# Weight copies issued one step later behind the attention's stores, and the order of seven products

## The chip, the cores and the metric

The kernel runs on one core of a Trainium2 chip. The metric is the device time of one execution in microseconds (us). Engines are named as in the profile: PE (matrix products), PEld (its weight loads), DVE and POOL (vector work), ACT (activations and copies) and SP, which in this kernel computes nothing and issues nearly all the DMA transfers, in the order in which they are written. L909 is line 909 of the kernel before.

## The reference

Two blocks follow each other. Attention keeps, of each row of scores, the 32 largest:

```python
scores = scale * q @ k.T                                  # 8 x 8 heads, 576 x 576, head size 64
mask   = scores >= (32nd largest of the row)
attn   = softmax(where(mask, scores, -1e9))
x      = (attn @ v), heads side by side                   # 8 x 576 x 512
```

Then comes a Fourier mixing and an MLP with two layers:

```python
u   = x + real(fft(fft(x, axis=1), axis=2))
un  = (u - mean(u)) / sqrt(var(u) + 1e-6)
out = u + relu(un @ w_ch1) @ w_ch2                        # 512 -> 2048 -> 512
```

All of it is float32; the output is 8 x 576 x 512.

## The kernel before

**Steps.** The attention is cut into 288 items (`items`, `N` = 288), each up to 128 rows of one head's scores; two heads form a pair, a pair has 9 items, and a batch element has 4 pairs, or 36 items. The loop at L1492 makes one step of each item. Step i does on DVE the 32-largest search of item i (eight passes, L425 and L427), on PE the scores of item i+3, and on ACT and POOL the masking of item i-1 (`mask`, L448 and L451) and its exponentials (`expo`, L459).

**P and its transposes.** The weights after the exponential are called P. For most pairs P is transposed by DMA: `plane` (called at L1560 and L1561 for item i-2) has ACT copy P into two planes of 16 bits (L472) and has SP store them in DRAM (L485, or L488 for the item of the tails); `turn` (L1557, for item i-3, every second item) has SP issue a DMA transpose from DRAM into the tile PT (L506). `attend` (L555, matmuls on L564) multiplies PT by v; it comes last of PE's work in its step. The result goes through ACT (`attended`), is turned back by PE in `to_tokens` (matmuls on L604) and normalised by DVE (L608). So DVE waits at L608 for everything that PE has in front of L604.

**The MLP rides along.** The MLP of a batch element runs in the steps of the next one, in units of about 1.75 us of PE, which a planner (`level`, `some`) puts between the fixed PE work of each step so that steps get about 6 us of PE work. The first layer is `hidden` (L966), the second is `back` (L986, matmuls on L993 for full tiles and L1032 for the tails).

**Seven products.** For batch elements 1 to 6 the second layer of the first two full row tiles, and in the last batch element that of all four, is made in `fast` (L1068) by seven half-size products in place of eight. h is split in four (11, 12, 21, 22) and the weight w2 in four blocks, of which the two off-diagonal ones (`w2_12`, `w2_21`) serve as places for ready-made combinations T1 to T4 of the blocks, kept in DRAM together with copies of the two blocks themselves (B12, B21). A product has two parts of 4 half-width matmuls (L1163, 1.75 us by the planner). `bring` (L906) issues the DMA on L909 that copies half of a combination (512 KB) from DRAM into one of the two places, in program order right after the product part that was the last to read that place. The products and what they bring are:

| product | reads | then brings |
|---|---|---|
| p2 | h12, w2_21 | T4 into w2_21 |
| p1 | h11, block 11 | nothing; puts `mix` of h11, and of h12, on a list for POOL |
| p5 | h21 (after a `mix`), T1 in w2_12 | T2 into w2_12 |
| p4 | h22, T4 in w2_21 | T3 into w2_21; puts `mix` of h22 on the list |
| p6 | mixed h11, T2 in w2_12 | B12 back into w2_12 |
| p3 | mixed h12, block 22 | nothing |
| p7 | mixed h22, T3 in w2_21 | B21 back into w2_21 |

After p7 the tails' second layer reads all of w2 (`back` with t = 4, four quarters b0 to b3, L1032): b0 and b1 read the first halves of the restored blocks, b2 and b3 the second. `mix` is a POOL subtraction (L1108, 1.28 us each); it is made when POOL has room at the end of a step (`some_sums`), or at once when a product asks for it (`need`).

**SP's order.** In step i SP gets: `turn` of item i-3, the store of item i-2, then the brings of the products made in this step, then loads of q, k or v (L240 to L288). Since SP works through its list in order, a bring that waits for its product holds up the loads and the next step's `turn` and store behind it.

Of the kernel before, what the change touches and what calls it, by code (L numbers as in the profile page):

```python
# [73 lines left out]
def kernel(  # L74
# [9 lines left out]
    nc = tc.nc  # L84
# [247 lines left out]
    N = len(items)  # L332
# [109 lines left out]
    def by_dma(i):  # L442
        return pair_by_dma(i // PER_PAIR)
# [22 lines left out]
    def plane(i, half):  # L466

        if not (0 <= i < N and by_dma(i)):
            return
        words = Wk[i].bitcast(U16).rearrange("p (h s) -> p h s", h=2)  # L470
        src = Ssb[i].bitcast(U16).rearrange("p (s h) -> p h s", h=2)
        nc.scalar.copy(out=words[:, half, :], in_=src[:, half, :])  # L472
        if half == 0:
            return
        Ssb.pop(i)
        Wk.pop(i)
        pair, t, e = items[i]
        nq = TAIL if e is None else P
        if e != 1:
            planes_of[pair, t] = dramp.tile(  # L480
                [nq, 2, 2 * S], U16, name=f"planes_{pair}_{t}", tag="planes", bufs=3
            )
        to = planes_of[pair, t]
        if e is not None:
            nc.sync.dma_start(out=to[:, :, S * e:S * (e + 1)], in_=words)  # L485
        else:
            for h in range(2):
                nc.sync.dma_start(  # L488
                    out=to[:, :, S * h:S * (h + 1)], in_=words[nq * h:nq * (h + 1)]
                )  # L490
        if e != 1:
            Wp.pop(i)
# [410 lines left out]
    scr = dramp.tile([P, len(OPS), NK, DH], F32, name="w2_parts", tag="w2_parts")  # L903
    w2_12, w2_21 = w2[:, 0:NK, DH:DM], w2[:, NK:NIT, 0:DH]

    def bring(o, place, part):  # L906
        kcs = slice(NK // 2 * part, NK // 2 * (part + 1))
        dst = place[part] if isinstance(place, list) else place[:, kcs]
        nc.sync.dma_start(out=dst, in_=scr[:, o, kcs, :])  # L909

    parts = {}

# [39 lines left out]
    def mlp_units(b):  # L952
# [115 lines left out]
        def fast(ch):  # L1068
# [109 lines left out]
            def p2(part):  # L1178
                c = product("v", lo, "12", lambda kc: w2_21[:, kc], part, True)
                if not last:  # L1180
                    bring(T4, second, part)
                if part:
                    to_x(ta, lo, c, 0)
# [8 lines left out]
            def p5(part):  # L1192
                need((b, ch, "21", part))
                c = product("v", hi, "21", first, part, False)
                bring(T2, w2_12, part)
                if part:
                    to_x(tb, hi, c, 2)

            def p4(part):

                c = product("z" if last else "w", hi, "22", in_second, part, last)
                bring(T3, second, part)
                if part:
                    to_x(tb, lo, c, 3, lambda: banks["z"][1]())
                    mix("22", "22", "11")
# [23 lines left out]
            def begin():  # L1229
# [6 lines left out]
                (0.0, lambda: mix("21", "21", "22", ALU.add), "back")  # L1236
            ] + [
                (1.75, lambda f=f, part=part: f(part), "back")
                for f in (p2, p1, p5, p4, p6, p3, p7) for part in range(2)
            ]  # L1240

        units = []
        for ch in range(2):
            units += [
                (8 * CW[ch] / 1200.0, lambda ch=ch, it=it: hidden(ch, it), "hidden")
                for it in range(NIT)
            ]
            seven = b and ch == 0 or last
            if seven:
                begin, products = fast(ch)  # L1250
                units.insert(1 - NIT, begin)
                units += products
            for t in [t for t in CHUNKS[ch] if t == 4 or not seven]:
                units += [
                    (1.75, lambda ch=ch, t=t, p=p: back(ch, t, p), "back")
                    for p in range(4 if t == 4 else 8)
                ]
# [114 lines left out]
    for o, place in ((B12, w2_12), (B21, w2_21)):  # L1372
        at(PER_BATCH + 14, "load2", lambda o=o, place=place: nc.sync.dma_start(
            out=scr[:, o], in_=place
# [62 lines left out]
        arrivals.append(s + (1 if quick else 2))  # L1437
        at(arrivals[-1], "units", lambda b=b: (queue if b else waiting).extend(mlp_units(b)))

    queue, waiting, pending, written, now, out_next = [], [], [], set(), [0], []  # L1440
    step_us = 6.0

    def chunk_at(i):
# [29 lines left out]
    def run(i, where):  # L1473
        for fn in plan.pop((i, where), []):
            fn()
# [16 lines left out]
    while i < N + 5 or plan or queue or sums:  # L1492
# [66 lines left out]
            mask(i - 1)  # L1559
        plane(i - 2, 0)  # L1560
        plane(i - 2, 1)  # L1561
        run(i, "convert")
        if short:
            expo(i - 1)
# [98 lines left out]
```

## Time and profile before

| | us |
|---|---|
| median of three runs | 1877.12 |
| lowest and highest of them | 1875.20 and 1878.28 |
| the profiled execution's own time | 1876.57 |
| its span from first to last instruction | 1874.8 |
| PE busy | 1703.8 (91%) |
| DVE busy | 1583.8 (84%) |
| ACT busy | 1295.0 (69%) |
| POOL busy | 912.5 (49%) |

The seven products of batch elements 1 to 6 stand at about 577 to 624, 806 to 837, 1008 to 1050, 1218 to 1257, 1423 to 1465 and 1629 to 1662 us of the span; those of the last one at 1787 to 1871. They are called stretches 1 to 7 from here on. A row of the timeline gives start, duration, engine, line, operation, tiles and count, and in brackets how long the engine was idle before and what ended that. Records of PE count a float32 matmul in two passes, so a product part shows as x8 and an `attend` of 10 matmuls as x20. SP's rows are issues, with the time that the issue took; the data land some us later. "PEclk" is the granted share of PE's clock.

### The profile page before, as it was taken

Reading aid. Unit: us, or ns where it says so; the run is one execution under the profiler, and the core shown is the slowest. Engines: PE = TensorE matmul, PEld = TensorE weight load, DVE = VectorE, ACT = ScalarE, POOL = GpSimd, SP = SyncE. Lnnn points to the kernel's source line nnn. Section 1 sums busy time; section 2 is a strip of 40 time slices with the busy share of each in tenths; the row PEclk is TensorE's granted clock in tenths of the full one; section 3 lists DMA queues with packets and bytes.
Section 4 is the critical chain, followed back from the end, with each engine's and each line's share of the span. In section 5 each row is a group of like instructions: output and inputs, shape, how many; then the busy total and the mean of one; then the engine's idle time right before and its main releaser. Section 6 shows DMA issues by size and latency. Waiting matters only on the chain.

```text
span 1874.8 us, 26903 instructions
## 1 busy us (share of the span) xinstructions
PE 1703.8 (91%) x8134; PEld 1086.4 (58%) x8134; DVE 1583.8 (84%) x3301; ACT 1295.0 (69%) x3104; POOL 912.5 (49%) x1278
## 2 busy tenths in 40 slices
PE   5566699789899899999999999989999999999999
PEld 3344465355466555666556565666567555677677
DVE  7999989888899999999999899899999899762110
ACT  6878659577788788877787678767787678652100
POOL 4768643454746266355545465255545364341012
PEclk7777799999999999999999999999999999999999
DMA  5333016661557755586466745694566645530132
GB/s 167 104 98 109 20 46 170 168 164 26 137 146 202 187 130 136 150 209 161 123 161 180 180 114 132 155 231 127 122 162 182 172 121 143 130 111 6 51 114 69
DMA packets 516576, 249.16 MB, mean 133 GB/s; under 512 B 398288, under 2 KB 506448, under 8 KB 516432
## 3 DMA queue, kind: packets, MB, share of 16 engines
q1 hardware_dynamic: 515664, 247.23, 50.9%
q8 instruction: 65, 1.06, 0.2%
q14 instruction: 79, 0.65, 0.1%
q10 hardware_dynamic: 768, 0.21, 0.0%
HBM read 93.63 MB, written 84.74 MB: 95 GB/s over the span
## 4 chain that ended last, share of the span: by engine, by line
PE 55%; DVE 13%; ACT 10%; POOL 10%; issue 6%; DMA 4%; SPq 2%; POOLq 0%; DVEq 0%; ACTq 0%
PE hp L966 22%; PE o L564 7%; DVE wk L427 6%; DVE m L425 6%; PE sp L401 4%; PE cp L993 4%; POOL wk L451 4%; PE cw L1163 3%; PE cv L1163 3%; PE cp L1032 3%; ACT wk L448 2%; POOL fg L651 2%; PE yp L755 2%; ACT wk L472 2%; PE sp_t L371 2%
## 5 line engine op out<-in xcount | busy, mean ns | idle before, releaser
L451 POOL TENSOR_TENSOR wk<-S,wk 128x576 f32<-128x576 f32 x288 | 408.1, 1417 | 549.8 <-ACT wk L448 533.9
L425 DVE MAX8 m<-wk 128x8 f32<-128x576 f32 x864 | 626.5, 749 | 6.2
L966 PE MATMUL hp<-unT,w 128*128 128x256 f32 (+1 forms) x2048 | 529.5, 411 | 5.2 <-ACT unT L884 2.7
L966 PEld LDWEIGHTS hp<-unT,w 128*128 128x128 f32 x2048 | 382.5, 192 | 116.5 <-issue 10.7
L427 DVE MATCH_REPLACE8 wk<-m,wk 128x576 f32<-128x576 f32 x576 | 427.4, 742 | 0.0
L472 ACT COPY wk<-S 128x576 uint16<-128x576 uint16 x468 | 289.1, 668 | 0.0
L448 ACT ACTIVATE wk<-S,nt 128x576 f32<-128x576 f32 x288 | 222.9, 774 | 85.4 <-POOL nt L434 84.5
L564 PE MATMUL o<-PT,v 128*64 128x256 f32 (+3 forms) x1440 | 204.8, 430 | 37.9 <-DMA PT<-planes 19.5
L993 PE MATMUL cp<-w,hT 128*128 128x512 f32 x512 | 236.4, 602 | 0.0
L425 DVE MAX8 m<-S 128x8 f32<-128x576 f32 x288 | 213.5, 741 | 7.8 <-ACT S L375 7.8
L459 ACT ACTIVATE S<-wk,nt 128x576 f32<-128x576 f32 x234 | 184.2, 787 | 48.3 <-POOL wk L451 47.2
L427 DVE MATCH_REPLACE8 wk<-m,S 128x576 f32<-128x576 f32 x288 | 213.5, 741 | 0.0
L970 ACT ACTIVATE hT<-hp 128x320 f32<-128x320 f32 (+1 forms) x256 | 103.9, 412 | 156.3 <-PE hp L966 155.2
L401 PE MATMUL sp<-kT,qT 64*128 64x512 f32 (+1 forms) x528 | 170.7, 676 | 24.2 <-ACT kT L318 9.4
L564 PEld LDWEIGHTS o<-PT,v 128*64 128x64 f32 x1440 | 117.9, 158 | 114.9 <-issue 37.0
L404 ACT COPY S<-sp 128x512 f32<-128x512 f32 (+1 forms) x264 | 141.6, 586 | 24.4 <-PE sp L401 23.3
L993 PEld LDWEIGHTS cp<-w,hT 128*128 128x128 f32 x512 | 93.4, 193 | 91.4 <-issue 91.0
L1108 POOL TENSOR_TENSOR hT<-hT 128x512 f32<-128x512 f32 x64 | 81.6, 1277 | 106.5 <-ACT hT L970 91.5
L434 POOL TENSOR_TENSOR nt<-m,cc 128x2 f32<-128x2 f32 x288 | 59.1, 205 | 126.2 <-DVE m L425 122.5
L371 PEld LDWEIGHTS sp_t<-kt,qT 128*128 128x128 f32 x320 | 51.3, 196 | 108.9 <-issue 70.0
L1163 PE MATMUL cw<-w,hT 128*128 128x256 f32 x448 | 105.0, 381 | 1.5 <-POOL hT L1108 0.9
L527 PE MATMUL tpP<-ident,wk 128*128 128x128 f32 x216 | 40.8, 320 | 61.1 <-ACT wk L459 36.1
(160 smaller groups left out, 2174.3 us busy)
## 6 DMA issues: line engine op xcount, KB each, us to landing
planes<-wk SPq DMA_DIRECT2D x208, 288.0 KB, 2.7
w<-w_parts SPq DMA_DIRECT2D x82, 512.0 KB, 4.7
space<-in_moe_w_ch_dram SPq DMA_DIRECT2D x32, 512.0 KB, 3.7
nat<-in_q_dram SPq DMA_DIRECT2D x128, 64.0 KB, 2.7
v<-in_v_dram SPq DMA_DIRECT2D x64, 128.0 KB, 3.0
out_dram<-x SPq DMA_DIRECT2D x32, 256.0 KB, 2.7
nat<-in_k_dram SPq DMA_DIRECT2D x62, 128.0 KB, 3.0
planes<-wk SPq DMA_DIRECT2D x52, 144.0 KB, 2.6
```

What stands on the lines that cost most here:

```text
L401: nc.tensor.matmul(sp[r], lhsT=qT[hd, q_cols], rhs=kT[hd, :], start=True, stop=True)
L404: nc.scalar.copy(out=s_t[r, keys], in_=sp[r])
L425: ops.append(lambda src=src, m8=m8: nc.vector.max(out=m8, in_=src))
L427: ops.append(lambda src=src, m8=m8: nc.vector.match_replace(w, m8, src, NEG))
L448: nc.scalar.activation(out=w, in_=Ssb[i], func=AF.Relu, scale=-FAR, bias=Nt[i][:, 1:2])
L451: nc.gpsimd.tensor_tensor(out=w, in0=Ssb[i], in1=w, op=ALU.subtract)
L459: nc.scalar.activation(out=Ssb[i] if by_dma(i) else w, in_=w, func=AF.Exp, bias=Nt.pop(i)[:, 0:1], accum_out=den_t[pair % 3][:, c:c + 1],)
L472: nc.scalar.copy(out=words[:, half, :], in_=src[:, half, :])
L564: nc.tensor.matmul(o[D * e:D * (e + 1), c0:c1], lhsT=vv[:, c, e, :], rhs=pt[:, NF if c == NF else (NF + 1) * e + c, c0:c1], start=(c == 0) ...
L966: nc.tensor.matmul(hp[:, 0:w], lhsT=w1[:, dt, P * it:P * (it + 1)], rhs=unT[:, dt, 0:w], start=(dt == 0), stop=(dt == NDT - 1),)
L993: nc.tensor.matmul(cp, lhsT=hT[:, it, P * n:P * (n + 1)], rhs=w2[:, it, :], start=(it == 0), stop=(it == NIT - 1),)
L1163: nc.tensor.matmul(dst, lhsT=h()[a][:, kc, :], rhs=rhs_of(kc), start=start and kc == 0, stop=kc == NK - 1, skip_group_check=True,)
```

## The change

`bring` no longer issues its DMA at once. While attention items are left (steps below 288) it puts the issue on a list, `brought`, and the next step issues what is on the list right after its own store of P. From step 288 on, which takes in the last batch element, it issues at once as before. The products' order goes from p2, p1, p5, p4, p6, p3, p7 to p2, p5, p1, p4, p6, p3, p7, for the last batch element too.

```diff
@@ bring
         kcs = slice(NK // 2 * part, NK // 2 * (part + 1))
         dst = place[part] if isinstance(place, list) else place[:, kcs]
-        nc.sync.dma_start(out=dst, in_=scr[:, o, kcs, :])
+
+        def go():
+            nc.sync.dma_start(out=dst, in_=scr[:, o, kcs, :])
+
+        if now[0] < N:
+            brought.append(go)
+        else:
+            go()
@@ fast
                 (1.75, lambda f=f, part=part: f(part), "back")
-                for f in (p2, p1, p5, p4, p6, p3, p7) for part in range(2)
+                for f in (p2, p5, p1, p4, p6, p3, p7) for part in range(2)
@@ the loop over the steps
         plane(i - 2, 0)
         plane(i - 2, 1)
+        for fn in brought:
+            fn()
+        brought.clear()
         run(i, "convert")
```

What this makes of the order in stretch 3, step by step ("turn" and "store" are SP's work for P, [..] a bring where it is issued, the others are PE's units; scores and transposes are left out; b0 to b3 are the tails' quarters):

```
step  before                                     after
174   store p2b [T4b] attend                     store [T4a] p2b attend
175   turn store p1a p1b p5a [T2a]               turn store [T4b] p5a p5b p1a
176   store p5b [T2b] p4a [T3a] tok p4b [T3b]    store [T2a] [T2b] p1b p4a tok p4b
177   turn store p6a [B12a] p6b [B12b]           turn store [T3a] [T3b] p6a p6b
178   turn store p3a p3b p7a [B21a]              turn store [B12a] [B12b] p3a p3b p7a
179   store attend                               store [B21a] attend
180   turn store p7b [B21b] b0 b1                turn store p7b b0 b1
181   store b2 tok b3                            store [B21b] b2 tok b3
```

Stretches 4 and 5 have the same pattern. In stretch 1 the end is: attend, then a step with [B21a] p7b b0, then one with [B21b] b1 b2 tok b3. In stretch 2 both halves of B21 are issued in a step that ends with attend, and b0 follows in the next. In stretch 6 the pair at hand is transposed on PE, so the last steps have no turn and no store, and stretch 7 has no attention beside it.

More of the change, by code (lines that the diff above doesn't have):

```diff
@@ L1438 @@
         at(arrivals[-1], "units", lambda b=b: (queue if b else waiting).extend(mlp_units(b)))
-    queue, waiting, pending, written, now, out_next = [], [], [], set(), [0], []
+    queue, waiting, pending, written, now, out_next, brought = [], [], [], set(), [0], [], []
     step_us = 6.0
```

## The prediction

> **What bounds the kernel now.** I read the page's first two parts, then the waits of PE and DVE from 500 to 1720 us, then the timelines of SP, PE and ACT around the stretches.
>
> ```profile
> PE 1703.8 (91%) x8134; PEld 1086.4 (58%) x8134; DVE 1583.8 (84%) x3301; ACT 1295.0 (69%) x3104; POOL 912.5 (49%) x1278
> PE   5566699789899899999999999989999999999999
> DVE  7999989888899999999999899899999899762110
> ```
>
> From a quarter of the span on, PE and DVE are both full: a microsecond is won only where both get it. So I looked for places where PE stalls and DVE then waits for PE. The windows over stretches 1 to 6 (235 us together) have PE busy 217.3 and DVE 226.4; PE's losses are these:
>
> ```profile
> PE o L564 <- DMA PT<-planes: 10.4, 3, 4.7
> PE o L564 <- DVE m L425: 6.1, 2, 4.3
> PE o L564 <- DVE x L1121: 4.5, 2, 2.8
> PE cp L1032 <- DMA w<-w_parts: 2.7, 2, 2.4
> DVE x L608 <- PE tpx L604: 54.6, 22, 6.7
> ```
>
> All but 1.8 of the first three rows' 21 us falls at `attend` in stretches 1 to 5: 1.84 and 4.70; 2.84; 3.88; 1.62; 4.29. The DVE names in the second and third row are only the last of several waits; the transposes landed then too. Some 12 to 16 us after each, DVE waits at L608 for PE: 2.45, 2.28, 5.43, 5.11, 4.93 us. In stretch 3:
>
> ```profile
> 1022.40 4.58 SPq L909 DMA_DIRECT2D w<-w_parts  x3
> 1027.03 2.04 SPq L240 DMA_DIRECT2D nat<-in_q_dram  x4
> 1029.11 0.94 SPq L279 DMA_DIRECT2D nat<-in_q_dram  x2
> 1030.09 2.88 SPq L506 DMA_TRANSPOSE PT<-planes  x1
> 1033.08 1.22 SPq L488 DMA_DIRECT2D planes<-wk  x2
> 1036.23 1.87 SPq L506 DMA_TRANSPOSE PT<-planes  x1
> ...
> 1042.06 5.60 PE L564 MATMUL o<-PT,v 128*64 128x320 f32 x20 [3.88 <-DMA PT<-planes]
> 1047.58 2.21 PE L1163 MATMUL cw<-w,hT 128*128 128x256 f32 x8
> 1049.72 1.94 PE L1032 MATMUL cp<-w,hT 128*64 128x512 f32 x8
> 1051.59 0.77 PE L308 MATMUL tpq<-ident,nat 128*128 128x128 f32 x5
> 1052.29 1.94 PE L1032 MATMUL cp<-w,hT 128*64 128x512 f32 x8
> ```
>
> SP sits in brings that wait for p5b, p4a and p4b until 1027, then issues q loads; the turn that could have gone out at about 1026 goes at 1030.09, the store behind it (ready on ACT at 1028.9) at 1033.08, the next turn at 1036.23. PE ends its scores at 1038.18 and waits for that turn.
>
> The rate after such a stall counts too:
>
> ```profile
> 1041.00:1048.00 7.00, 5.60 (x20) 2.43 (x20) 0.52 0.74 212
> 614.00:621.00 7.00, 4.54 (x20) 2.44 (x20) 0.54 1.03 235
> 1251.63 2.91 PE L564 MATMUL o<-PT,v 128*64 128x320 f32 x20 [1.62 <-DVE x L1121]
> ```
>
> After 3.88 us of idling the granted clock is 0.52 and the attend takes 5.60; after 1.62 it takes 2.91. (In the windows the clock is the third number from the end.) So a stall of about 4 us costs 1.4 (4.28 against 2.91, stretch 5) to 2.7 us on top.
>
> **The change, part 1: SP no longer waits for products.** Brings now wait for products of the step before, which are done. In stretch 3, T2a and T2b go out by 1023, the q loads by 1026, the turn at 1026 to 1029, the store at 1029 to 1030.2, T3a and T3b by 1031.4, the last turn at about 1032. Turns here land 4.1 to 5.6 us after issue (1016.71 to 1021.25, 1036.23 to 1041.81): 1037.6 at the latest, before 1038.2. The attend's 3.88 and its half clock go. The same shift takes out 4.29 in stretch 5, 1.62 in 4, 1.84 and all but about 1 of 4.70 in 1. In stretch 2 it takes 2.84, but T3a, which lands at 828.7 now, goes behind a store that ends at about 831.3 and lands at about 836; p7a, wanted at 833.5, waits 2.5, and with p7 (3.8) and the scores (1.6) the attend starts at 841.4, as now.
>
> **Part 2: the order.** p5 moves ahead of p1, so T2 has two units more to arrive. p5 needs the mix of h21, which ends at 580.4, 810.1, 1010.9, 1221.2, 1426.7 on POOL; p5 would start at 582.2, 809.6 (its first half needs only the one that ended at 808.7) and 1015 or later: covered. The mixes behind p1 come a step later. p6 and p3 still find theirs (POOL's places of that step, 1021.66 to 1025.9 and 1029.21 to 1031.9, end before 1027.9 and about 1031.4); but the mix of h22 is now asked for by p7a itself, behind the mask's POOL row that ends at 1034.18, plus 1.28: 1035.5 against 1034.8. That is +0.7 for stretches 3, 4, 5, bounds 0 and 1.4. In stretch 7 PE alone works; h21's second mix ends at 1789.03, p5 would start at 1790.6, h11's and h12's mixes start 3.4 later and end by about 1801.5, and p6 needs h11 at 1801: nothing lost, nothing gained. Stretch 6 has no stall at PE and hardly any store for SP to wait on: nothing.
>
> **Part 3: what is late next.** B21b is read by b2. Before, it is issued right after p7b. Now it is issued a step later, behind a store that waits for ACT, and ACT works in order: its copies of the q transposes come before the mask and the planes. In stretch 3:
>
> ```profile
> 1052.29 0.71 ACT L316 ACTIVATE qT<-tpq 128x512 f32<-128x512 f32 x2 [3.52 <-PE tpq L308]
> 1053.64 0.77 ACT L448 ACTIVATE wk<-S,nt 128x576 f32<-128x576 f32 x1
> 1054.31 1.24 ACT L472 COPY wk<-S 128x576 uint16<-128x576 uint16 x2
> ```
>
> From PE's tpq to the planes' end are 3.3 us (1052.29 to 1055.55), the store's issue takes 0.6, and a bring lands 4.5 after its issue (1050.88 to 1055.20 and 1466.01 to 1470.50; bounds 3.7, the shortest of the 82, and 5.9, 1258.95 to 1264.88). So b2 cannot run before about 8.3 us after tpq; between them PE has 2.6 us of work (b1 1.94, scores 0.66). A new wait of 5.7 us stands after tpq, wherever tpq is, ahead of L604 for which DVE waits. Now:
> - Stretch 3: attend at 1038.2 + 0.7, + 2.9, p7b 1.9, b0 1.9, tpq 0.8: 1046.3. Plus 8.3: 1054.7, where b2 today got its weights at 1055.20: -0.4.
> - Stretch 5: 1454.0 + 0.7 + 7.5 + 8.3 = 1470.5, today 1470.50: 0.
> - Stretch 4: 1250.0 + 0.7 + 7.5 + 8.3 = 1266.5, today 1264.9 (a wait of 2.43 there already): +1.6.
> - Stretch 1: the store before B21a is ready when ACT ends at 617.8, so B21a lands at 617.8 + 0.6 + 4.6 = 623.0; b0 runs at 624.07 today. B21b follows a DVE-paced step of 5.1 later: 628.0, against 628.35: -0.3.
> - Stretch 2: both land by about 845, b0 is wanted at 844.3 and ran at 844.16: +0.8.
>
> Sum +1.7. Then the clock: the new waits of 5.7 to 6.7 us in stretches 1, 3, 4, 5 are longer than the 3.88 after which it halved. Up to L604 PE has 2.5 us of work (b2 1.94, tpx 0.55), at 1.5 to 1.9 times its duration by the attends (4.28 and 5.60 over 2.91): +1.2 to +2.2, I take 1.6, four times: +6.4. The Trainium skill ("TensorE: Matmul & The Clock Gate", "What's actually happening") has the clock halve after an idle window of about 3.4 us and return after a busy one of the same length. By that rule a wait would lose at most 1.7 us and the four together 6.8; the trace's own attends lost between 1.4 and 2.7 each, which reaches past it.
>
> **Sum:** +1.7 + 6.4 = +8.1 on the profiled execution's 1876.57 (span 1874.8), which is 0.55 below the median: 1877.1 + 8 = 1885. The removed waits are worth about 17, and nearly all of it is given back at b2.
>
> **Rivals.**
> - *The brings are in time* (faster). DVE's five waits shrink by what PE wins: 2.45, 2.28, 5.4, 1.6 to 4.1, 4.9, that is 16.7 to 19: 1859. For it: each such wait follows a stall at attend. Against it: it needs B21b to land within 2.6 us of tpq, and the row of ACT alone takes 3.3. Half of it, 1868, if landings take 3.7 and the clock stays up. Together 0.20. It decides from the point at which the store of that step is issued ahead of tpq.
> - *Attend still waits* (much slower). The brings now go out between store and turn and share the DMA engines with both: the store of 604.84, behind two brings, landed in 5.3 instead of 2.5. If attend keeps 2 to 4 us of its wait, tpq moves back and b2 with it, one to one: 5 times 2 more, 1895. For it: the DMA share is 0.83 to 0.92 in the stretches. Against it: in stretch 3 the turn goes out 4 us earlier than today, more than the 2.8 by which that store was late. 0.17.
> - *Nothing moves* (within 0.2%). The new waits equal the old ones in place and the clock's loss is not on DVE's path: +1.7 or less, 1878. 0.18.
>
> The forecast itself, +4 to +14: 0.45.
>
> **Numbers.** Bounds of the forecast: landing 3.7 and no p7a wait, -0.8 and -0.7 a stretch, clock +1.2: about 1878; landing 5.9 and clock 2.2: 1893. The range reaches over half of the faster rival and the slower one's centre: 1866 to 1897. A measurement of this kernel tells about 0.2% (3.8 us) from no change. Faster 0.20, same 0.18, slower 0.62.
>
> **What would show it.** Right: no or short waits at L564 for the turn in stretches 1 to 5, L1032 waiting for w_parts by 4 to 7 us four times, a clock near 0.5 behind each, and DVE's waits at L608 as long as now. Wrong in part 1: the attends wait on. Wrong in part 3: L1032 waits under 2 us and L608 shrinks. SP's L909 should hardly wait for PE at all before 1660.

## The result, and the profile after

The changed kernel takes 1910.24 us, median of four runs (1908.90 to 1915.44), against 1877.70 for the kernel before beside it: a ratio of 1.0179, with an interval from 1.0166 to 1.0192. The forecast was slower, by 8 us; it became 32.5. The profiled execution took 1908.90 us, its span is 1907.1: 32.3 more than the span before.

The first row of the page, the engines' busy time:

```profile
PE 1715.9 (90%) x8134; PEld 1085.6 (57%) x8134; DVE 1585.2 (83%) x3301; ACT 1294.3 (68%) x3104; POOL 912.3 (48%) x1278
```

No engine has more work (DVE 1585.2 against 1583.8); only PE has 12 us more busy time, of the same 8134 instructions: the 256 matmul records of the tails' second layer (L1032, now L1039) alone went from 64.1 to 78.9 us. That is a lower clock, not work, as the rows below show. The waits of PE and DVE from 500 to 1720 us (total, times, longest):

```profile
PE cp L1039 <- DMA w<-w_parts: 30.2, 9, 8.8
...
PE cw L1170 <- DMA w<-w_parts: 5.1, 3, 2.2
...
PE cw L1170 <- POOL hT L1115: 2.7, 3, 1.8
PE o L564 <- DMA PT<-planes: 2.5, 2, 1.5
...
DVE x L608 <- PE tpx L604: 78.5, 20, 10.9
```

`attend` (L564) waited 21 us before and waits 2.5 for its turns now, and 1.9 once for DVE: what the change was to remove is gone. But b0 and b2 (L1039, L1032 before) waited 2.7 and wait 30.2, and DVE's wait at L608 grows from 54.6 to 78.5. Stretch 3 on SP and PE:

```profile
1046.56 1.84 SPq L506 DMA_TRANSPOSE PT<-planes  x1
...
1049.17 1.36 SPq L911 DMA_DIRECT2D w<-w_parts  x2
1050.58 1.20 SPq L288 DMA_DIRECT2D v<-in_v_dram  x2
1051.82 1.96 SPq L255 DMA_DIRECT2D v<-in_v_dram  x2
1053.89 0.60 SPq L485 DMA_DIRECT2D planes<-wk  x1
1054.59 0.56 SPq L911 DMA_DIRECT2D w<-w_parts  x1
...
1066.26 0.55 SPq L485 DMA_DIRECT2D planes<-wk  x1
1066.86 0.60 SPq L911 DMA_DIRECT2D w<-w_parts  x1
```

```profile
1049.45 1.97 PE L1170 MATMUL cw<-w,hT 128*128 128x256 f32 x8 [1.77 <-POOL hT L1115]
...
1052.83 2.91 PE L564 MATMUL o<-PT,v 128*64 128x320 f32 x20
...
1057.60 1.07 PE L1039 MATMUL cp<-w,hT 128*64 128x512 f32 x2
1060.39 1.93 PE L1039 MATMUL cp<-w,hT 128*64 128x512 f32 x6 [1.72 <-DMA w<-w_parts]
1062.25 0.76 PE L308 MATMUL tpq<-ident,nat 128*128 128x128 f32 x5
...
1065.40 1.07 PE L1039 MATMUL cp<-w,hT 128*64 128x512 f32 x2
1071.51 3.62 PE L1039 MATMUL cp<-w,hT 128*64 128x512 f32 x6 [5.03 <-DMA w<-w_parts]
```

The attend at 1052.83 waits for nothing and takes 2.91 (5.60 before). Then come two waits. b0 wants B21a, which SP issues at 1054.59, behind a turn, a store, two brings, four v loads and another store, and which lands 5.8 us later: 1.72 us of waiting, and b0 is cut in two pieces. b2 wants B21b, issued at 1066.86 behind the store of that step: 5.03 us, and its last six records take 3.62. The same six took 1.93 in the kernel before, in stretch 4 after a shorter wait:

```profile
1264.92 1.93 PE L1032 MATMUL cp<-w,hT 128*64 128x512 f32 x6 [2.43 <-DMA w<-w_parts]
```

Stretches 4 and 5 have b2 waits of 5.07 and 4.77 now, and a granted clock (third number from the end) of 0.50 behind them; here stretch 4:

```profile
1284.00:1289.00 5.00, 4.74 (x11) 1.51 (x13) 0.19 (x1) 0.00 (x0) 0.00 (x0) 0.50 0.59 125
```

In stretch 1 b0 waits 8.80, in stretch 2 2.22.

How far each stretch moves is best read at the end of its wait at L608 (the start of DVE's add there), counted from the first product of the stretch:

| stretch | 1 | 2 | 3 | 4 | 5 | sum |
|---|---|---|---|---|---|---|
| before, us | 53.65 | 47.59 | 49.64 | 48.65 | 49.15 | |
| after, us | 59.79 | 53.28 | 55.16 | 55.25 | 54.72 | |
| later by | 6.1 | 5.7 | 5.5 | 6.6 | 5.6 | 29.5 |
| predicted (b2 or b0, and clock) | 1.3 | 0.8 | 1.2 | 3.2 | 1.6 | 8.1 |

Stretch 6, to the end of p7, grows from 33.1 to 34.7 us (by 1.5 unrounded) and stretch 7 from 83.8 to 85.1. 29.5 + 1.5 + 1.3 = 32.3 is the whole difference of the spans. The parts between the stretches change too, by -3.1 to +1.9 us each, but cancel in the sum.

### The profile page after: what moved, and what is told of

It is laid out like the page before. It is cut to its first block, busy times and chain, and to the rows that moved or that the text cites. A ratio compares the mean times of both kernels' runs of the same rounds, so it can differ in the third digit from the quotient of the medians.

```text
span 1907.1 us, 26916 instructions
## 1 busy us (share of the span) xinstructions
PE 1715.9 (90%) x8134; PEld 1085.6 (57%) x8134; DVE 1585.2 (83%) x3301; ACT 1294.3 (68%) x3104; POOL 912.3 (48%) x1278
## 4 chain that ended last, share of the span: by engine, by line
PE 55%; ACT 12%; POOL 11%; DVE 7%; DMA 6%; issue 6%; SPq 3%; POOLq 0%; ACTq 0%; DVEq 0%
PE hp L973 22%; PE o L564 6%; POOL wk L451 4%; PE sp L401 4%; PE cp L1000 4%; PE cw L1170 3%; PE cv L1170 3%; DVE m L425 3%; PE cp L1039 3%; ACT wk L448 3%; DVE wk L427 3%; PE yp L755 2%; POOL fg L651 2%; DMA w<-w_parts 2%; ACT wk L472 2%
## 5 line engine op out<-in xcount | busy, mean ns | idle before, releaser
L564 PE MATMUL o<-PT,v 128*64 128x256 f32 (+3 forms) x1440 | 200.3, 423 | 21.1 <-DMA PT<-planes 11.5
L564 PEld LDWEIGHTS o<-PT,v 128*64 128x64 f32 x1440 | 115.4, 156 | 96.5 <-issue 30.5
L1039 PE MATMUL cp<-w,hT 128*64 128x512 f32 x256 | 78.9, 670 | 30.2 <-DMA w<-w_parts 30.2
```

The source lines that it names most:

```text
L564: nc.tensor.matmul(o[D * e:D * (e + 1), c0:c1], lhsT=vv[:, c, e, :], rhs=pt[:, NF if c == NF else (NF + 1) * e + c, c0:c1], start=(c == 0) ...
```

## The experiments

All ratios are to the kernel before, run beside the experiment on the same chip (its medians lie between 1874.46 and 1877.23). At that reading 0.001 is 1.9 us.

### The two parts of the change, each alone

Deferral with the old order of products:

```diff
-                for f in (p2, p5, p1, p4, p6, p3, p7) for part in range(2)
+                for f in (p2, p1, p5, p4, p6, p3, p7) for part in range(2)
```

> Every bring deferred by a step, the products in the old order. Theory A (the return of B21 is what comes late: the quarters b0 and b2 of the tails wait for it, and the order costs next to nothing): the time stays near the changed kernel's, 1905 +- 4, with L1032's counterpart waiting about 5 us for w_parts in stretches 3, 4 and 5 and 8 to 9 in stretch 1. Theory B (the order costs: T and the mixes come late for p6 and p7): near 1880, as the old order is back.

Measured: 1915.33, ratio 1.0210 (1.0193 to 1.0227). That is slower than theory A's range, and far from theory B. Two of PE's waits in stretch 3:

```profile
1043.47 3.54 PE L1170 MATMUL cw<-w,hT 128*128 128x256 f32 x8 [4.76 <-DMA w<-w_parts]
...
1071.92 3.67 PE L1039 MATMUL cp<-w,hT 128*64 128x512 f32 x6 [5.04 <-DMA w<-w_parts]
```

The new order does what it says within the deferral: without it p6 waits 4.76 us for T2. Yet it is worth only some 6 us (0.0031); b0's and b2's waits are there with both orders (b2's 5.04, 4.82 and 5.30 in stretches 3 to 5 here).

The new order, with the brings issued at once:

```diff
-        if now[0] < N:
+        if False:
```

> Brings at once as before, the products in the new order. Theory A: 1880 +- 4, within 0.4% of the kernel before; the attends wait for their turns as before. Theory B: 1895 to 1910, with PE waiting for POOL's mixes or for T at L1163's counterpart.

Measured: 1880.71, ratio 1.0031 (1.0019 to 1.0043). The attends still wait (2.78, 2.90, 2.44, 1.17 and 2.87 us), and stretches 6 and 7 are 34.7 and 85.1 us, exactly as in the changed kernel. So the order by itself costs a little, and the deferral is where the 33 us come from.

### Is it B21?

The changed kernel with B21 issued at once by SP:

```diff
-        if now[0] < N:
+        if now[0] < N and o != B21:
```

> The changed kernel, but the return of B21 issued at once behind p7, all other brings deferred, new order. Theory A: the waits of the tails' quarters fall to under 2 us, the attends stay without a wait, DVE's waits at L608 fall under 4 us a stretch: 1865 +- 6, faster than the kernel before. Theory C (any deferred bring crowds the DMA engines behind the store and delays stores and turns): 1890 to 1905, waits move to the attends.

Measured: 1888.90, ratio 1.0072 (1.0056 to 1.0087): far above the 1865 that B21's lateness alone had promised, though 0.0107 of the 0.0179 is gone. Theory C's waits at the attends didn't come either (4.2 us in all at L564). Most of what is left stands at the tails, where PE waits 16.0 us for B21. "At once" in the program isn't at once on SP, as its queue and PE show in stretch 3:

```profile
1039.89 0.60 SPq L485 DMA_DIRECT2D planes<-wk  x1
1045.22 2.85 SPq L506 DMA_TRANSPOSE PT<-planes  x1
1048.17 0.61 SPq L485 DMA_DIRECT2D planes<-wk  x1
1048.87 0.56 SPq L911 DMA_DIRECT2D w<-w_parts  x1
```

```profile
1053.46 3.67 PE L1039 MATMUL cp<-w,hT 128*64 128x512 f32 x6 [4.97 <-DMA w<-w_parts]
```

B21b is free to go when p7b ends at 1042.4 on PE, but SP stands at the turn of 1045.22 until the store of 1039.89 has landed (5.3 us after its issue), and then does turn and store: 6.5 us lost in the queue. In the kernel before, that turn was late too (1047.46), but so was p7b.

The kernel before with only B21 deferred, in the old order:

```diff
-        if now[0] < N:
+        if now[0] < N and o == B21:
...
-                for f in (p2, p5, p1, p4, p6, p3, p7) for part in range(2)
+                for f in (p2, p1, p5, p4, p6, p3, p7) for part in range(2)
```

> The kernel before with only the return of B21 deferred, old order. Theory A: the attends wait as before (1.6 to 4.7 us each), and the quarter b2 then waits on top of it, since its 8.3 us run from PE's q transposes: 5 to 8 us more a stretch in four stretches, 1900 to 1915. Theory C: 1880 to 1888, as 12 of 72 deferred brings crowd little.

Measured: 1895.98, ratio 1.0113 (1.0098 to 1.0128), a little under the lower end of what was expected. Here both waits stand in one stretch (3):

```profile
1044.64 5.39 PE L564 MATMUL o<-PT,v 128*64 128x320 f32 x20 [3.91 <-DMA PT<-planes]
...
1062.76 3.68 PE L1039 MATMUL cp<-w,hT 128*64 128x512 f32 x6 [4.78 <-DMA w<-w_parts]
```

A late B21 alone costs 21 us, and gives nothing back at the attends. It is the largest single part, not the whole.

### B21 past SP's queue

The changed kernel, B21 issued at once by ACT:

```diff
-            nc.sync.dma_start(out=dst, in_=scr[:, o, kcs, :])
+            (nc.scalar if o == B21 and now[0] < N else nc.sync).dma_start(out=dst, in_=scr[:, o, kcs, :])
-        if now[0] < N:
+        if now[0] < N and o != B21:
```

> As the run with B21 at once, but the two halves of B21 are issued by ACT, not SP, behind p7's parts; all other brings deferred on SP, new order. Theory A2 (with B21 at once the quarter b2 still waits 3 to 5 us because SP reaches the issue only behind a turn that waits for its store to land; SP's own queue for P is the floor that the removed waits run into): ACT has nothing to wait for but p7b, B21b lands about 5 us after it, before b2; the waits for w_parts at the tails go, and DVE's waits at L608 fall under 3 us: 1868 +- 6. Theory D (the transfers themselves are slow, whoever issues them): b2 still waits 3 us or more, 1885 +- 5.

Measured: 1869.11, ratio 0.9966 (0.9953 to 0.9979): as expected, and below both kernels. ACT issues B21b within 1 us of p7b's end at 1045.85, and b2 no longer waits, nor has it a slow clock (ACT, then PE's b0 and b2, stretch 3):

```profile
1046.65 0.37 ACTq L911 DMA_DIRECT2D w<-w_parts  x1
```

```profile
1047.94 1.93 PE L1039 MATMUL cp<-w,hT 128*64 128x512 f32 x6 [1.08 <-DMA w<-w_parts]
...
1052.95 1.94 PE L1039 MATMUL cp<-w,hT 128*64 128x512 f32 x8
```

```profile
DVE x L608 <- PE tpx L604: 37.7, 19, 5.8
```

DVE's wait at L608, 78.5 in the changed kernel and 54.6 before, is 37.7. Against the kernel with B21 at once on SP only the queue of one combination differs, and that is worth 19.8 us.

The Trainium skill ("DMA: Bandwidth & Descriptors", "Issuing engines are not separate DMA queues") says that issuing from several engines saves only the time of the sequencer, usually small beside the DMA itself. The landing agrees that nothing is won there: over stretches 1 to 5 B21's ten halves took 7.3 us from ACT's issue at the median (3.8 to 8.4), SP's 48 brings 5.2. But the sequencer's time isn't small where the sequencer stands at a semaphore in between: 6.5 us in stretch 3 of the run above, with B21 at once on SP.

Is it enough to take ACT as the queue? The kernel before, in the old order, with all brings at once on ACT, and then with only B21 there:

```diff
-        nc.sync.dma_start(out=dst, in_=scr[:, o, kcs, :])
+        (nc.scalar if now[0] < N else nc.sync).dma_start(out=dst, in_=scr[:, o, kcs, :])
```

> The kernel before, old order, brings at once, but all issued by ACT. Theory A2: SP's list holds P, loads and stores of the output alone, the turns go out as early as the stores land, the attends' waits fall from 19 us in all to under 6: 1862 +- 8. Against it: ACT waits in order for each product part, so the exponentials and the planes behind come up to 4 us later in the steps with brings; if those waits reach DVE or the turns, 1878 to 1895.

```diff
-        nc.sync.dma_start(out=dst, in_=scr[:, o, kcs, :])
+        (nc.scalar if o == B21 and now[0] < N else nc.sync).dma_start(out=dst, in_=scr[:, o, kcs, :])
```

> The kernel before with only B21 issued by ACT, at once. Theory A2: the attends wait as before, b2's 2.4 in stretch 4 goes: 1874 +- 4, near the kernel before. If B21 in SP's list is what delays the turns, 1868 or less.

Measured: 1880.57, ratio 1.0035 (1.0015 to 1.0055), and 1882.52, ratio 1.0040 (1.0024 to 1.0056). The first falls into the second of its two cases, the second lies above both of its own: no gain. The attends pay: they wait 18.1 and 25.9 us in stretches 1 to 5, 19.2 in the kernel before. In stretch 3 of the two (all brings, then B21 alone):

```profile
1047.44 5.60 PE L564 MATMUL o<-PT,v 128*64 128x320 f32 x20 [3.58 <-DMA PT<-planes]
```

```profile
1049.06 4.28 PE L564 MATMUL o<-PT,v 128*64 128x320 f32 x20 [7.88 <-DMA PT<-planes]
```

With B21 alone on ACT its turn is issued at 1038.86, 27.8 us into the stretch, right behind B12a and B12b, and lands in 10.0 us; in the changed kernel with B21 on ACT the turn of that place is issued at 1034.26, 26.1 us into it, and lands in 5.7. That the deferral is what gets the turn there before the attend needs it is read from these rows; the new order with B21 on ACT and nothing deferred was not run.

Does the new order of products matter to that? The other combinations deferred and B21 on ACT, in the old order:

```diff
-                for f in (p2, p5, p1, p4, p6, p3, p7) for part in range(2)
+                for f in (p2, p1, p5, p4, p6, p3, p7) for part in range(2)
```

> The other combinations deferred, B21 issued at once by ACT, but the old order of products in all stretches. If the new order is a needed part of what B21 on ACT wins (without it p6 waits 3.3 to 4.8 us for T2 in stretches 3 to 5, as in the deferral with the old order, less about 2.9 us that the new order costs in stretches 6 and 7): 1872 to 1880. If the deferral and ACT's queue alone carry it: 1865 to 1868.

Measured: 1881.99, ratio 1.0025 (1.0013 to 1.0037): the first case, and slightly above its range. PE's waits for combinations from 560 to 1720 us:

```profile
PE cw L1170 <- DMA w<-w_parts: 20.6, 5, 5.0
```

In the new order the same row had 5.3 from 500 to 1720 us. Five stretches have p6 waiting 3.44 to 5.03 us for T2. DVE's wait at L608 is even lower here, 34.9; the loss reaches DVE another way, at POOL's additions of the products' results, which come late with p6:

```profile
DVE x L1128 <- POOL x L1142: 24.1, 4, 6.6
```

In the new order that row had 6.6. So B21 on ACT needs the new order for T2, and, by the reading above, the deferral for the turns.

### Bytes or order of issue?

The changed kernel, every bring before step 288 copying the first quarter of its bytes (the output is incomplete):

```diff
-            nc.sync.dma_start(out=dst, in_=scr[:, o, kcs, :])
+            d, s = dst, scr[:, o, kcs, :]
+            if now[0] < N:
+                d, s = dst[:, 0:1], scr[:, o, kcs, :][:, 0:1]
+            nc.sync.dma_start(out=d, in_=s)
```

> The changed kernel with every bring before step 288 copying a quarter of its bytes (so part of the second layer's weights keep what stood there: left out to make the transfers short). Theory A (order of issue: the return is issued late behind store and ACT): b2's wait after the q transposes shrinks only by the shorter landing, from 5.0 to about 3 us, and the time by 10 to 15 of the 33. Theory D (bytes crowd the DMA engines): the waits go nearly all, 1880 or less.

Measured: 1873.58, ratio 1.0002 (0.9987 to 1.0016). With the issues where the change puts them, and less to carry, the loss is gone, as theory D had it; the waits are not: PE still waits 12.8 us for B21 (30.2 in the changed kernel). And the same with B21 whole, only the other copies small:

```diff
-            if now[0] < N:
+            if now[0] < N and o != B21:
```

> The changed kernel, but the copies of T1, T2, T3 and B12 that go out before step 288 carry only the first of their four column blocks, a quarter of the bytes; B21 is copied whole (the output is incomplete for it). Theory D (in the changed kernel the other copies' bytes stand ahead of stores, turns and B21, and make them land late): nearly all of what quarter copies of everything won stays, 1876 to 1884; b0 waits under 1 us for B21a in stretches 2 to 5, B21b lands about 4.5 us after its issue and b2 waits 4.5 to 5. Theory B (it is B21's own 512 KB that take the time): b0 and b2 wait as in the changed kernel, b0 by 1.7 and more, and the time is 1895 to 1908.

Measured: 1894.86, ratio 1.0106 (1.0092 to 1.0121), just under the one case and 11 above the other: neither. The waits fell out nearly as the first case had them (b0 still 1.24 in stretch 2), the time did not. The issues and median landings from 1005 to 1075 us, of the changed kernel and of this one:

```profile
w<-w_parts SPq DMA_DIRECT2D x10, 512.0 KB, 5.3
...
nat<-in_q_dram SPq DMA_DIRECT2D x4, 64.0 KB, 5.0
v<-in_v_dram SPq DMA_DIRECT2D x2, 128.0 KB, 5.8
```

```profile
w<-w_parts SPq DMA_DIRECT2D x8, 128.0 KB, 2.5
w<-w_parts SPq DMA_DIRECT2D x2, 512.0 KB, 4.5
...
nat<-in_q_dram SPq DMA_DIRECT2D x4, 64.0 KB, 2.1
v<-in_v_dram SPq DMA_DIRECT2D x2, 128.0 KB, 2.7
```

The same 64 KB of q take 5.0 us behind whole copies and 2.1 behind quarters; with all brings small those of B21 land in 2.5 to 2.7 as well. And PE in stretch 3, with B21 whole, and with all small:

```profile
1057.28 3.67 PE L1042 MATMUL cp<-w,hT 128*64 128x512 f32 x6 [4.91 <-DMA w<-w_parts]
```

```profile
1049.10 3.48 PE L1042 MATMUL cp<-w,hT 128*64 128x512 f32 x6 [3.15 <-DMA w<-w_parts]
```

b0 took 4.72, 4.73 and 3.69 us in stretches 3 to 5 of the changed kernel; it takes 3.11, 2.70 and 2.70 when the other copies are small, and 1.94, its bare duration, when all are. b2's wait of 4.9 to 5.1 stays until B21 is small too, and is then 3.0 to 3.2. Taken away in this order, the bytes of T1 to T3 and B12 are worth 0.0073 (14 us) and B21's own 0.0104 (20 us). These are prices of bytes in the changed order, not shares of what the change lost: the kernel before carries the same bytes (its q loads take 4.8 us in the same window), and it wasn't run with small copies. What they do show is that the landing of B21a behind other copies, which the prediction's sum didn't have, costs time there.

### The order in stretches 6 and 7, and T3

The kernel with B21 on ACT, and the old order in the last two stretches:

```diff
-                for f in (p2, p5, p1, p4, p6, p3, p7) for part in range(2)
+                for f in ((p2, p5, p1, p4, p6, p3, p7) if b < 6
+                          else (p2, p1, p5, p4, p6, p3, p7)) for part in range(2)
```

> The kernel of the changed order with B21 on ACT's queue, but stretches 6 and 7 in the old order of products. Theory O (the new order itself costs time where no attend waits: p5 there asks for the mix of h21 before POOL has it, and PE waits 0.70 and 0.69 us for it): stretches 6 and 7 go from 34.7 and 85.1 us back to about 33.1 and 83.8, and the time from 1869.1 to 1866.2, within 1.5. Rival (the two stretches are longer for where the copies are issued, not for the order): they stay at 34.7 and 85.1, and the time at 1869.

Measured: 1866.48, ratio 0.9958 (0.9941 to 0.9974), the lowest of all. The stretches go back to 33.1 and 84.1 us (33.1 and 83.8 in the kernel before); the gain in time, 2.6 us, is of the expected size, but its interval overlaps that of the kernel without this edit. The order causes the growth, by another way than was written there. In the changed kernel's stretch 7, PE, POOL and DVE:

```profile
1818.05 3.62 PE L1170 MATMUL cv<-w,hT 128*128 128x256 f32 x16
1822.36 3.69 PE L1170 MATMUL cv<-w,hT 128*128 128x256 f32 x16 [0.69 <-issue]
```

```profile
1818.76 1.27 POOL L1115 TENSOR_TENSOR hT<-hT 128x512 f32<-128x512 f32 x1 [7.34 <-ACT hT L977]
```

```profile
1821.77 0.48 DVE L1128 SCALAR_TENSOR_TENSOR x<-cv,gi,x 128x256 f32<-128x256 f32 x1 [37.22 <-PE cv L1170]
```

The mix has ended at 1820.03, but p5 starts 2.3 us later, right after DVE has read p2's result (1821.77 + 0.48 = 1822.25). p2 and p5 write the two halves of one PSUM tile, cv; p1, which stood between them, writes cw. The second half of that stretch has the same, 0.62, and 0.69 + 0.62 is the 1.3 by which it grew. That the shared tile is the reason is read from these rows; giving p5 another tile wasn't tried.

T3 on ACT as well:

```diff
-            (nc.scalar if o == B21 and now[0] < N else nc.sync).dma_start(out=dst, in_=scr[:, o, kcs, :])
+            (nc.scalar if o in (B21, T3) and now[0] < N else nc.sync).dma_start(out=dst, in_=scr[:, o, kcs, :])
-        if now[0] < N and o != B21:
+        if now[0] < N and o not in (B21, T3):
```

> As the kernel with the old order in stretches 6 and 7, but T3 too is issued at once by ACT. p7a waits 1.19, 2.32 and 1.83 us for T3a's landing in stretches 2, 3 and 5 when SP issues it. Theory S (T3 was late because SP stood in a store or turn): these waits go, and 3 to 5 us with them, 1862. Theory A (ACT, which would wait for p4a and p4b in its own order, makes the planes, the stores and the turns behind them late, as with all copies on ACT): attends wait again by 1 to 3 us, and the time is 1868 to 1874.

Measured: 1880.90, ratio 1.0033 (1.0020 to 1.0046); the second case, and worse than it. p7a's waits for T3 go, and the attends' come back (PE's waits from 560 to 1500 us):

```profile
PE o L564 <- DMA PT<-planes: 14.1, 5, 4.1
```

In stretch 3 ACT issues T3b at 1025.85, when p4b is done, and makes the next planes from 1027.31 on; the last turn ahead of the attend goes at 1036.17, 29.2 us into the stretch, where it went at 25.8 in the run just above, with T3 on SP. That ACT's wait for p4 is what holds up the planes is the reading of these rows; no run separates it.

## Why the prediction was wrong in size

Right, by its own steps:
- *Part 1.* The attends' waits and half clock go (0 in stretches 3 to 5, 1.51 in 1).
- *The chain of part 3.* "b2 cannot run before about 8.3 us after tpq": measured 8.5, 8.5 and 8.3 in stretches 3, 4 and 5.
- *The clock.* 1.6 each: from b2's restart to the end of the wait at L608 take 4.1, 4.5 and 4.5 us in stretches 3 to 5 instead of 2.5, so 1.6 to 2.1.
- *The sign*, and where the loss reaches DVE: 29.5 of the 32.3 us have been added by the end of its wait at L608 in stretches 1 to 5.

Wrong: the terms that place tpq, and with it the chain. The step that failed is part 3's "attend at 1038.2 + 0.7, + 2.9, p7b 1.9, b0 1.9, tpq 0.8", and the same sum for stretches 4 and 5. By stretch, in us later than that sum:

| term | 3 | 4 | 5 |
|---|---|---|---|
| attend's start (p7a behind the mix of h22, or behind T3a) | 1.5 | 0.0 | 1.9 |
| from attend to tpq: b0, taken as 1.9 | 2.7 | 2.7 | 1.7 |
| from tpq to b2 | 0.2 | 0.2 | -0.1 |
| clock, beyond 1.6 | 0.0 | 0.5 | 0.5 |
| sum | 4.4 | 3.4 | 4.0 |
| measured less predicted at L608 | 4.3 | 3.4 | 4.0 |

Of the 24 us by which the sum was too small, these three stretches hold 11.7, stretches 1 and 2 9.7, stretches 6 and 7 2.9.

- *b0.* B21a's landing was followed in stretches 1 and 2 only; in 3 to 5 b0 was entered with its bare duration. There B21a goes out behind brings and v loads, and lands 5.8 us after its issue in stretch 3; with the other copies small, 4.6, and b0 takes 1.6 us less.
- *p7a.* +0.7 was taken for the mix, with 1.4 as the bound. In stretch 3 p7a waits 1.77 for it, in stretch 5 2.22 for T3a, of which the sum had nothing.
- *Stretch 1.* "so B21a lands at 617.8 + 0.6 + 4.6 = 623.0": it lands at 628.4. SP was not there. A store of 612.89, right behind B12a and B12b, took 7.8 us to land, the turn behind it went at 620.77, the next store at 623.23 and B21a at 623.88:

```profile
611.62 1.16 SPq L911 DMA_DIRECT2D w<-w_parts  x2
612.89 0.56 SPq L485 DMA_DIRECT2D planes<-wk  x1
620.77 2.35 SPq L506 DMA_TRANSPOSE PT<-planes  x1
623.23 0.56 SPq L485 DMA_DIRECT2D planes<-wk  x1
623.88 0.56 SPq L911 DMA_DIRECT2D w<-w_parts  x1
```

- *Stretch 2.* B21a was to land at about 845, and lands at 855.3 in a stretch that itself starts 6.8 later: 3.5 too late, with p7a's 2.03 ahead of it. b0's last 14 records then take 5.34 us instead of 3.65 after a wait of only 2.22; the sum had no slow clock in this stretch.
- *Part 2.* In stretch 7 "nothing lost", in stretch 6 "nothing": +1.3 and +1.5. And p5, called "covered", waits 1.36 and 0.66 us in stretches 1 and 2, again with p2 right ahead of it.

Of the rivals, "attend still waits" had the right cause, brings that share the DMA engines with stores and turns, and even the row that sizes it (a store that landed in 5.3 instead of 2.5), but looked for its price at the attend alone. The turns bore it, though with less in hand than the 4 us argued there: in stretch 3 the last turn, issued at 1046.56, lands 5.2 later, 1.1 us ahead of the attend. B21a, behind the same copies, had nothing in hand.

## What to carry to other kernels

When transfers are moved behind others, walk each one of them to its reader, with the landing that it has behind its new neighbours, in every stretch; a reader entered at its bare duration is a transfer costed at nothing. "Issued at once" holds for the program, not for a queue that stands at a semaphore: the time that the sequencer stands there belongs to the landing, and another engine's queue can be worth more than another order, if that engine's own wait doesn't delay what the first queue waits for. Parts that lose one by one (the order alone +0.3%, the deferral alone +2.1%, B21 on ACT alone +0.4%) can win together (-0.3%).

## What the runs showed of the hardware

- Two 512 KB copies right ahead on the queue make the landing of a smaller transfer about twice as long or more: q loads of 64 KB 5.0 us against 2.1 behind copies of 128 KB, v loads of 128 KB 5.8 against 2.7, a store 7.8 against the stores' median of 2.7.
- PE's clock after a wait. Over these kernels, the last six records of b0 or b2 took 1.93 us after every wait up to 2.43, 1.93 after one of 2.97 and 3.36 after one of 3.07, and 2.85 to 3.68 after every longer one. But an attend of 20 records took 4.47 instead of 2.91 after only 2.44, and 14 records of b0 5.34 instead of 3.65 after only 2.11. The Trainium skill ("TensorE: Matmul & The Clock Gate", "What's actually happening") has the clock halve after at least one idle window of about 3.4 us, of a free-running kind: waits of 2.1 to 3.2 us already showed the slow rate here, some of them and not others.
